# Transposes of the last layer's tokens in four PSUM banks, and the places of some splits and joins in the queues of an attention, experts and MLP kernel

## The chip, the core and the metric

The kernel runs as one program on one core of a Trainium2 chip. The core has a matrix engine (TensorE: PE for matmuls and transposes, PEld for loading the stationary operand), a vector engine (DVE), a scalar engine (ACT), GpSimd (POOL) and SyncE (SP), which here issues nearly all plain DMAs. Each engine works through its own queue in program order; semaphores make one wait for another. A matmul writes to a PSUM bank of 128 x 512 float32. The metric is the time of one execution on the device in microseconds (us), as the median of several.

## The reference: what is computed

Three layers follow one another. Attention over (batch 4, heads 8, 768 positions, 64 wide) with 4 sink keys and a window of 128:

```
keep = is_sink | in_window
a = softmax(where(keep, q @ k.T / 8, -1e9));  x = a @ v     # 3072 tokens x 512
```

Then a mixture of 8 experts, in which each token with `x @ w_skip > 0` goes to the expert with the largest logit, and its result is added to the token:

```
h = relu(x[mask] @ w1[e]);  out[mask] = x[mask] + gate_w * (h @ w2[e])     # 512 -> 1024 -> 512
```

Last an MLP over all 3072 tokens:

```
h = x @ w_in;  r = relu(h);  g = r * r;  return g @ w_out     # 512 -> 2048 -> 512
```

The kernel keeps float32 accuracy by splitting each operand into a high part (rounded by a cast on ACT) and a low part (the difference, by a subtraction on DVE), and by summing three products: high x high, low x high, high x low.

## The kernel before

**Attention (up to about 225 us)** writes its tokens, in blocks of 128, to a buffer in DRAM, `xbuf`. While its last blocks finish, the early expert `e` is worked on in the same queues; the string `Z['chain']` gives the order of all these steps. In it `g0` to `g15` are quarters of the first matmul of `e`, `h0` to `h3` quarters of its second, `m` prepares one part of an expert's weights (`pump(1)`: cast on ACT, subtraction on DVE, then the next weight load on SP), `P` joins the token numbers of the next block on DVE and starts its gather on POOL. The chain ends at a branch on all engines (`tc.If(odd_v > 0)`, line 1102) that is not taken.

**The experts (264 to 424 us)** come in pairs, `units`: a `Pair` has 256 tokens, a `Block` 128. A unit gathers its rows from `xbuf` (`gather`, POOL), transposes them on PE and splits them (`tx`), multiplies with w1 (`g1`), transposes the result where it is a `Block` (`th`, tiles `tph`, `b_hh`, `b_hl`), multiplies with w2 (`g2`), adds the tokens on DVE (L220) and scatters them back to `xbuf` on POOL (L222) in `store`. Between these calls `pump(n)` puts n weight parts into the queues of ACT and DVE. In the last loop `u0` is the pair E-2, `u1` the block E-1, and `u2` one more block of an early expert.

**The MLP.** Its weights come packed as int64 words. `turn(u)` moves a short line of weight tiles on by one step each: `guard` (DVE), `low` (DVE), `begin` (DVE and ACT), `join` (DVE and ACT), `add` (POOL), `high` (ACT). The tail of the experts is ordered by `Z['tail']`: `G`, `a`, `b` are first matmuls of `u2`, `h` and `k` its transposes, `p` and `q` its second matmul, `t` a `turn()` without a new tile, `l` the load of weight tile 3, `u` `turn(wi[3])`, and `0` to `3` `transpose_x(0, t)`.

The MLP takes the tokens in six groups k of 512, the last group of `xbuf` first. `load_x(k, t)` reads 128 tokens from `xbuf`, `transpose_x(k, t)` transposes them by four PE transposes into one PSUM bank (`tpm`) and splits them in two halves of 128 x 256: cast c=0, subtraction c=0, cast c=1, subtraction c=1. The loads of group 1 stand behind the store of `u2`, since they read what it writes. The first steps are the products of weight tile f with group k, in the order (f, 0) for f = 0 to 3, then (0, k), (1, k) for k = 1 to 5; step s is one `gemm1` of 12 matmuls (L1313), a relu on ACT (L1319), a product on DVE (L1321) and a store. The dictionaries `before` and `after` hang loads and transposes on a step. After step 10 no transposes are left; the rest of the 96 steps and the second matmul (L1365) follow.

PSUM has eight banks of which each tile asks for one by a tag: `sc` has four, `tp` two, `xa` and `xb` one each. A tile whose bank is still being read waits for its readers.

Of the kernel before, what the change touches and what calls it, by code (L numbers as in the profile page):

```python
# [20 lines left out]
P = 128  # L21
B, H, S, D = 4, 8, 768, 64
N, DM, E, FF, DFF = 3072, 512, 8, 1024, 2048
# [21 lines left out]
TINY2 = float.fromhex("0x1.2p-15") ** 2  # L45
G = 512

Z = {'la': [0, 0, 2, 2, 7, 10, 12], 'lb': [4, 5, 14, 16, 19, 22, 24], 'ch': 25, 'rk': 35, 'pl': 36, 'ga': [34, 46, 47, 49], 'rw': [28, 29, 46, 54, 62, 70], 'ro': 53, 'rs': 12, 'rg': 4, 'sc0': 50, 'sc1': 0, 'sc2': 57, 'sc3': 12, 'fc': 47, 's2': 51, 'ei': [-5, -3], 'er': [5, 5], 'p': [3, 10], 'qd': [192, 288], 'lv': 31, 'F': [4, 7, 8, 11, 13], 'A': [0, 8, 1, 0, 0, 4], 'T': [1, 2, 6, 2, 1, 2], 'N': [3, 5, 8], 'chain': 't8 la4 lb0 lb2 la5 la6 lb1 lb3 etx r0 lb4 g0 r3 t9 lb5 lb6 r1 c0 c1 c2 c3 ga0 c4 c5 g1 rk ga1 ga2 p0 p2 p3 p4 ga3 r2 p1 p5 o0 s0 s2 s1 g2 o1 t10 s3 o2 s4 g3 rank o3 N0 s5 g4 R0 i0 N2 t11 g5 g6 g7 g8 g9 g10 X N1 i1 g11 g12 send P g13 g14 h0 g15 m m h1 O m m h2 m P m m m u0 m m i2 h3', 'tail': 'Gathbltpku0123q', 'S': [7, 14, 5], 'qd2': [480, 288], 'lv2': 15, 'e0': 3, 'p2': [3, 8], 'eg': 0}
NG = N // G
NF = DFF // P  # L50

# [2 lines left out]
def attn_moe_mlp(ctx: ExitStack, tc: tile.TileContext, kq, v, vs, n_sink, window, wl, w1, w2, w_in, w_out, out):  # L54
# [16 lines left out]
    def bank(tag, name):  # L71
        return ps.tile([P, 512], F32, name=name, tag=tag, bufs={"sc": 4, "tp": 2}.get(tag, 1))
# [8 lines left out]
    def row_tile(name):  # L81
        return wk.tile([P, DM], F32, name=name, tag="row", bufs=5)
# [19 lines left out]
    def join_ids(loaded):  # L102
        ids, n = loaded
        for k in range(1, TABS):
            nc.vector.tensor_tensor(out=ids[:, 0, 0:n], in0=ids[:, 0, 0:n], in1=ids[:, k, 0:n], op=ALU.bitwise_xor)
        return ids[:, 0]

    def split(dst_hi, dst_lo, src):

        nc.scalar.copy(dst_hi, src)  # L110
        nc.vector.tensor_tensor(out=dst_lo, in0=src, in1=dst_hi.bitcast(F32), op=ALU.subtract)  # L111
# [173 lines left out]
    with tc.manual_schedule():  # L285
# [45 lines left out]
        ei = ac.tile([P, 3, E], I32, name="ei")  # L331
# [412 lines left out]
        def at(t, f, p=PTS - 1):  # L744

            plan.setdefault((t + p // PTS, p % PTS), []).append(f)
# [5 lines left out]
        def plan_finish(b, t):  # L752
# [3 lines left out]
            for fs, ps in (  # L756
                (la, Z['la']), (lb, Z['lb']), (choose, range(Z['ch'], Z['ch'] + 6)), ([rank], (Z['rk'],)),
                (place, range(Z['pl'], Z['pl'] + 6)), (gate, Z['ga']),
            ):
                for f, p in zip(fs, ps, strict=True):  # L760
                    at(t, f, p)
            for k, (f, g) in enumerate(rws):
                p = Z['rw'][k] if b == B - 2 else Z['ro'] + Z['rs'] * k
                at(t, f, p)
                at(t, g, p + Z['rg'])
            for k, f in enumerate(scat):
                at(t, f, Z['sc0'] + Z['sc1'] * k if b == B - 2 else Z['sc2'] + Z['sc3'] * k)
# [15 lines left out]
        for n in range(1, B * NP):  # L783
            t, a = n * NQ, (n // NP, n % NP)
# [9 lines left out]
        for t in range(len(units) + 4):  # L794
# [84 lines left out]
        def prep():  # L879

            r = seq[len(units)]
            if r == E:
                units.append(Block(eids[1], 0, etiles, EROWS))
            else:
                ids = ids_of[r] = join_ids(ids_of[r])
                if r in seq[0:3]:

                    own = ids[:, 0:ALLOC[r], 0]
                    nc.vector.tensor_scalar(own, own, nowhere, None, op0=ALU.max)
                units.append(Pair(ids, chunk) if ALLOC[r] == 2 else Block(ids, 0, etiles if len(units) == E - 1 else single_tiles))  # L890
            return units[-1]
# [9 lines left out]
        def send(most=10):  # L901
            while sent[0] < min(len(parts), most - sent[0] % 2):
                r, i = parts[sent[0]]
                if r not in wts_of:
                    if r < E:
                        regs(r)
                    wts_of[r] = Expert(wpa if seq.index(r) % 2 else wpb, e_r[r] if r < E else ew[1], stage)
                wts_of[r].load(i)
                sent[0] += 2

        def pump(n):
            for k in range(n):
# [14 lines left out]
        g1 = [lambda c=c, p=p: e.g1(w_e, c, p, 4) for c in range(4) for p in range(4)]  # L927
        g2 = [lambda p=p: e.g2(w_e, p, 4, False) for p in range(4)]
# [236 lines left out]
        wi = [Unpack(True, f) for f in range(NF)]  # L1165
# [3 lines left out]
        def turn(u=None, between=None):  # L1169

            line.append(u)
            if line[-3]:
                line[-3].guard()
            if line[-4]:
                line[-4].low()
            if u:
                u.begin()
            if between:
                between()
            if u:  # L1180
                u.join()
            if line[-2]:
                line[-2].add()
            if line[-3]:
                line[-3].high()
# [3 lines left out]
        def x_tile(k, a, c):  # L1189
            if k < 2:  # L1190
                return big_tile(4 * k + 3 + 2 * a + c, "xt", F32R)
            return wpb.tile([P, 2, 512], F32R, name=f"w{4 * (k - 2) + 2 * a + c}")

        def load_x(k, t):
            r0 = order[k] * G + t * P
            xgs[k, t] = row_tile("xg") if k == 0 else wpa.tile([P, DM], F32, name="xg", tag=f"w{8 + 4 * (k % 2) + t}")
            nc.sync.dma_start(xgs[k, t], xbuf[r0:r0 + P, :])

        def transpose_x(k, t):
            if t == 0:  # L1200
                xts[k] = [[x_tile(k, a, c) for c in range(2)] for a in range(2)]
            xg = xgs.pop((k, t))
            tp = bank(("sc", "xa", "tp", "tp")[t] if k == 0 else "xa" if t % 2 else "xb", "tpm").rearrange("p (k c) -> p k c", k=4)
            for c in range(4):
                nc.tensor.transpose(tp[:, c, :], xg[:, c * P:(c + 1) * P], ident)  # L1205
            for c in range(2):
                split(xts[k][0][c][:, :, t * P:(t + 1) * P], xts[k][1][c][:, :, t * P:(t + 1) * P], tp[:, 2 * c:2 * c + 2])

        order = [NG - 1] + list(range(NG - 1))
        def wt(n):  # L1210
            return wts_of[seq[n]]

        for n in range(0, E - 2, 2):
            u0, u1 = units[n], units[n + 1]
# [29 lines left out]
        u0, u1, u2 = units[E - 2], units[E - 1], None  # L1244
        for c in range(4):
            u0.g1(wt(E - 2), c)
            pump(4)
            if c == 2:
                u1.tx()
        prep()  # L1250
        for c in range(2):
            u1.g1(wt(E - 1), c)
# [13 lines left out]
        turn(wi[0])  # L1266
        u2.tx()
        u1.g2(wt(E - 1), 1, 2)
        turn(wi[1])
        turn(wi[2])  # L1270
        u1.store()
        for t in range(4):
            load_x(0, t)
        acts = {
            "G": lambda: u2.g1(wt(E), 0), "a": lambda: u2.g1(wt(E), 1, 0, 2), "b": lambda: u2.g1(wt(E), 1, 1, 2),
            "h": lambda: u2.th(0), "k": lambda: u2.th(1), "p": lambda: u2.g2(wt(E), 0, 2, "xb"), "q": lambda: u2.g2(wt(E), 1, 2, "xb"),
# [7 lines left out]
        before, after = {}, {}  # L1284

        def on(when, s, f):
            when.setdefault(s, []).append(f)

        on(before, 0, u2.store)
        for k in range(1, NG):  # L1290
            for t in range(4):
                on(before, 0 if k == 1 else 2 * k - 2, lambda k=k, t=t: load_x(k, t))
                on(after, 2 * k if k > 1 else 2, lambda k=k, t=t: transpose_x(k, t))

        enter = []
        for f in range(4, NF):
# [59 lines left out]
        for s in range(BEHIND, len(steps) + 2 * LOADS):  # L1356
            if s - 2 * LOADS >= 0:
                k, f = steps[s - 2 * LOADS]
# [8 lines left out]
                if f == NF - 1:  # L1367
                    for t in range(4):
# [8 lines left out]
                        r0 = order[k] * G + t * P  # L1377
# [54 lines left out]
```

## Time and profile before

| | us |
|---|---|
| median of 3 runs | 998.36 (996.07 to 1000.64) |
| the profiled execution | 999.1 |
| its span, first to last instruction | 997.4 |
| PE busy | 947.2 (95% of the span) |
| DVE busy | 531.3 (53%) |
| ACT busy | 436.2 (44%) |
| POOL busy | 126.7 (13%) |

The chain of work that ended last is 67% PE; it starts at the branch, at 264.5 us. PE has few gaps left: the profile's 40 slices show it below 90% at three places, the start, the stretch around the branch, and the change from the experts to the MLP at 400 to 490 us. From 491.72 us on PE is busy to the end. In the rows below, a row of the timeline gives start, duration, engine, line, operation, output<-inputs, shapes, count, and in brackets the idle time of the engine before it and who ended it. `SPq` is a DMA being issued, `PEclk` the granted clock of TensorE as a share of full speed.

### The profile page before, as it was taken

What the parts mean: (1) busy time and instruction counts of PE and PEld (TensorE: products, weight loads), DVE (VectorE), ACT (ScalarE), POOL (GpSimd) and SP (SyncE); (2) the same over time, 40 slices, a digit from 0 to 9 for tenths busy, and PEclk for the clock granted to TensorE, in tenths of its full rate; (3) what the DMA queues carried; (4) which work ended last, traced back from release to release, by engine and by line L of the source; (5) the groups of instructions that cost most, each with busy time, mean ns of one, the idle gap of its engine ahead of it and who ended that gap; (6) DMA issues with size and microseconds to landing.
All of it is one profiled execution on the core that took longest, in us unless ns stands there. A gap on an engine that the chain in (4) does not pass through costs nothing.

```text
span 997.4 us, 15187 instructions
## 1 busy us (share of the span) xinstructions
PE 947.2 (95%) x5259; PEld 744.2 (75%) x5259; DVE 531.3 (53%) x1269; ACT 436.2 (44%) x1031; POOL 126.7 (13%) x186
## 2 busy tenths in 40 slices
PE   7999999977799999978799999999999999999998
PEld 4666666657589888756688888888888888888886
DVE  6566677845598798744464555555332232323231
ACT  5766666743276465533443444444232222222221
POOL 3101112122212211200021212112000000000000
PEclk9999999989799999999999999999999999999999
DMA  5433545543698888355354544454353443434231
GB/s 178 146 105 100 145 143 147 177 102 107 221 311 269 287 291 285 133 159 173 110 185 142 176 160 158 154 176 155 116 189 86 149 144 91 144 91 141 85 127 43
DMA packets 90408, 157.17 MB, mean 158 GB/s; under 512 B 14630, under 2 KB 35750, under 8 KB 90322
## 3 DMA queue, kind: packets, MB, share of 16 engines
q1 hardware_dynamic: 87154, 149.11, 46.6%
q0 software_dynamic: 3168, 7.01, 2.1%
q8 instruction: 43, 0.70, 0.3%
q14 instruction: 43, 0.35, 0.1%
HBM read 114.67 MB, written 42.30 MB: 157 GB/s over the span
## 4 chain that ended last, share of the span: by engine, by line
PE 67%; DVE 2%; issue 2%; ACT 1%; DMA 1%; POOL 0%; SPq 0%; POOLq 0%; DVEq 0%; ACTq 0%
PE hpm L1313 27%; PE acc L1365 26%; PE yp L275 4%; PE hp L257 4%; PE hp L197 2%; PE yp L217 2%; PE tpm L1205 1%; DVE w L145 1%; DMA w<-in_w_in_dram 1%; PE tph L206 0%; DVE xt L111 0%; PE tpx L244 0%; ACT xt L110 0%; DVE ua L1140 0%; DVE ua L1146 0%
## 5 line engine op out<-in xcount | busy, mean ns | idle before, releaser
L1365 PE MATMUL acc<-w,gs 128*128 128x512 f32 x1152 | 263.8, 391 | 0.0
L1365 PEld LDWEIGHTS acc<-w,gs 128*128 128x128 f32 x1152 | 216.3, 188 | 47.4
L1313 PE MATMUL hpm<-w,wi 128*128 128x512 f32 x720 | 171.0, 396 | 0.0
L111 DVE TENSOR_TENSOR gs<-g,gs 128x512 fp32r<-128x512 f32 x96 | 66.3, 693 | 177.0 <-ACT gs L110 177.0
L1313 PEld LDWEIGHTS hpm<-w,wi 128*128 128x128 f32 x720 | 135.1, 188 | 32.4
L110 ACT CAST gs<-g 128x512 fp32r<-128x512 f32 x96 | 59.2, 619 | 184.2 <-PE acc L1365 183.7
L1321 DVE SCALAR_TENSOR_TENSOR r<-hpm,r 128x512 f32<-128x512 f32 x96 | 66.3, 691 | 134.1 <-ACT r L1319 134.1
L1319 ACT ACTIVATE r<-hpm 128x512 f32<-128x512 f32 x96 | 57.4, 598 | 165.0 <-PE hpm L1313 165.0
L145 DVE TENSOR_TENSOR w<-wst,w 128x512 fp32r<-128x512 f32 x160 | 103.4, 687 | 16.0 <-ACT w L141 14.9
L468 DVE CUSTOM_DVE_ANT_0 pt<-sc,m 128x272 f32<-128x272 f32 (+2 forms) x192 | 73.4, 409 | 52.5 <-PE sc L457 37.5
L477 ACT ACTIVATE pt<-pt,nm 128x272 f32<-128x272 f32 (+2 forms) x192 | 94.0, 493 | 5.5 <-DVE nm L468 5.5
L141 ACT CAST w<-wst 128x512 fp32r<-128x512 f32 x142 | 81.1, 620 | 25.7 <-DMA wst<-in_w_dram 17.5
L1313 PE MATMUL hpm<-xt,wi 128*128 128x512 f32 x360 | 89.3, 404 | 3.0 <-ACT xt L110 3.0
L1313 PEld LDWEIGHTS hpm<-xt,wi 128*128 128x128 f32 x360 | 69.3, 193 | 20.3 <-ACT xt L110 3.4
L457 PE MATMUL sc<-kq 64*128 64x272 f32 (+2 forms) x384 | 68.1, 433 | 6.0 <-DMA kq<-in_kq_dram 5.9
L1151 POOL TENSOR_TENSOR ua<-ua,ur 128x512 uint32<-128x512 uint32 x32 | 44.6, 1394 | 227.8 <-DVE ua L1146 178.4
L540 PE MATMUL xacc<-pT,vt 128*64 128x128 f32 x704 | 60.4, 289 | 2.6 <-DMA vt<-in_v_dram 1.5
L512 PE MATMUL tp<-ident,pt 128*128 128x128 f32 x352 | 59.1, 287 | 0.0
L512 PEld LDWEIGHTS tp<-ident,pt 128*128 128x128 f32 x352 | 38.2, 142 | 26.2 <-ACT pt L477 12.2
L540 PEld LDWEIGHTS xacc<-pT,vt 128*64 128x64 f32 x704 | 37.1, 137 | 19.3 <-issue 14.3
L257 PE MATMUL hp<-x,w 128*128 128x256 f32 x384 | 47.7, 282 | 0.4 <-DVE x L111 0.4
L257 PEld LDWEIGHTS hp<-x,w 128*128 128x128 f32 x384 | 46.6, 188 | 1.0 <-DVE x L111 0.7
(226 smaller groups left out, 1043.1 us busy)
## 6 DMA issues: line engine op xcount, KB each, us to landing
wst<-in_w_dram SPq DMA_DIRECT2D x80, 512.0 KB, 4.9
gbuf<-r SPq DMA_DIRECT2D x96, 256.0 KB, 2.1
g<-gbuf SPq DMA_DIRECT2D x48, 512.0 KB, 3.7
kq<-in_kq_dram SPq DMA_DIRECT2D x15, 800.0 KB, 4.7
w<-in_w_out_dram SPq DMA_DIRECT2D x16, 512.0 KB, 3.8
wi<-in_w_in_dram SPq DMA_DIRECT2D x15, 512.0 KB, 4.6
vt<-in_v_dram SPq DMA_DIRECT2D x16, 384.0 KB, 5.2
xbuf<-x_sb SPq DMA_DIRECT2D x24, 256.0 KB, 4.4
```

The source lines that it names most:

```text
L111: nc.vector.tensor_tensor(out=dst_lo, in0=src, in1=dst_hi.bitcast(F32), op=ALU.subtract)
L141: copy(self.s[i][:, 0], self.raw[i])
L145: eng.tensor_tensor(out=s[:, 1], in0=self.raw.pop(i), in1=s.bitcast(F32)[:, 0], op=ALU.subtract)
L257: nc.tensor.matmul(self.hp[:, f * 2 * P:(f + 1) * 2 * P], wt.s[c // 2 * 4 + k][:, b, col:col + P], self.x[k // 2][a][:, k % 2 * 2 * P:(k % ...
L457: nc.tensor.matmul(sc[:, 0:wn], kq_sb[own, KW + i * P:KW + (i + 1) * P], kq_sb[own, k0:k0 + wn], start=True, stop=True)
L468: nc.vector.tensor_tensor_reduce(out=pt[:, h, 0:wn], in0=score[u][h][:, 0:wn], in1=(m0, m1, m2)[min(i, 2)], scale=-0.125, scalar=3.0e38, o ...
L477: nc.scalar.activation(out=pt[:, h, 0:wn], in_=pt[:, h, 0:wn], func=AF.Exp, bias=nm[:, h:h + 1], scale=-1.0, accum_out=ssum[:, b, 2 * pr + ...
L512: nc.tensor.transpose(tp[:, h, j, :], pt[:, h, c0:c0 + P], ident)
L540: nc.tensor.matmul(x[h * D:h * D + D, c * P:(c + 1) * P], vv[:, jb, h * D:h * D + D], pT[:, h, j, :], start=j == 0 and (own or first), sto ...
L1313: nc.tensor.matmul(hp, w[:, a, c], x[c // 2][:, c % 2], start=n == 0, stop=n == 11)
L1321: turn(u, lambda: nc.vector.scalar_tensor_tensor(out=r, in0=hp, scalar=0.0, in1=r, op0=ALU.max, op1=ALU.mult))
L1365: nc.tensor.matmul(acc[k][t], g[:, a, t * P:(t + 1) * P], w[:, b], start=f == 0 and n == 0, stop=f == NF - 1 and n == 2)
```

## The change

Six edits, all of order or of place; no arithmetic changes.

```diff
-Z = {... 'chain': '... g12 send P g13 g14 h0 g15 m m h1 O m m h2 ...', 'tail': 'Gathbltpku0123q', ...}
+Z = {... 'chain': '... g12 send g13 g14 g15 h0 m m P h1 O m m h2 ...', 'tail': 'Gathbltpk0123uq', ...}
...
-            tp = bank(("sc", "xa", "tp", "tp")[t] if k == 0 else "xa" if t % 2 else "xb", "tpm").rearrange("p (k c) -> p k c", k=4)
+            tp = bank("sc" if k == 0 and t == 0 else ("xb", "xa", "tp", "tp")[t], "tpm").rearrange("p (k c) -> p k c", k=4)
...
             u0.g1(wt(E - 2), c)
-            pump(4)
             if c == 2:
                 u1.tx()
+            pump(4)
...
             u0.g2(wt(E - 2), p, 4)
-            if p == 1:
+            if p == 0:
                 u1.th(0)
                 u1.th(1)
             pump(6)
...
         u1.g2(wt(E - 1), 1, 2)
-        turn(wi[1])
-        turn(wi[2])
         u1.store()
         for t in range(4):
             load_x(0, t)
+        turn(wi[1])
+        turn(wi[2])
...
-                on(after, 2 * k if k > 1 else 2, lambda k=k, t=t: transpose_x(k, t))
+                on(after, 2 if k == 1 else 2 * k - 1 + t // 2, lambda k=k, t=t: transpose_x(k, t))
```

The transposes of groups 2 to 5 now stand two by two behind two steps in a row, and each of the four tiles of a group has a bank of its own. On PE, before, from the last step of group 0 with three others around it (`x16` are the 16 transposes of one group):

```order
L1313 MATMUL hpm<-xt,wi 128x512 x36
L1205 MATMUL tpm<-ident,xg 128x128 x16
L1313 MATMUL hpm<-xt,w_11977 128x512 x12
L1313 MATMUL hpm<-xt,wi 128x512 x12
L1205 MATMUL tpm<-ident,xg 128x128 x16
L1313 MATMUL hpm<-xt,wi 128x512 x12
```

And in the changed kernel at the same place:

```order
L1313 MATMUL hpm<-xt,wi 128x512 x36
L1205 MATMUL tpm<-ident,xg 128x128 x16
L1313 MATMUL hpm<-xt,w_11977 128x512 x12
L1205 MATMUL tpm<-ident,xg 128x128 x8
L1313 MATMUL hpm<-xt,wi 128x512 x12
L1205 MATMUL tpm<-ident,xg 128x128 x8
L1313 MATMUL hpm<-xt,wi 128x512 x12
L1205 MATMUL tpm<-ident,xg 128x128 x8
```

Group 1 keeps its 16 in one piece; group 2 comes in two pieces of 8, the first of them one step earlier. On DVE, in the tail of the experts, before, from the low part of the tokens of `u2` (`b_xl`) to the low part of its first transposed half (`b_hl`); L1140 and L1146 are `begin` and `join`, L1155 `guard`, L1162 `low`, L220 the add of `u1`'s store:

```order
L111 TENSOR_TENSOR b_xl<-tpx,b_xh 128x512
L1140 TENSOR_SCALAR ua<-wi 128x512
L1146 SCALAR_TENSOR_TENSOR ua<-wi,ua 128x512
L1155 SCALAR_TENSOR_TENSOR ua<-sq,ua 128x512
L1140 TENSOR_SCALAR ua<-wi 128x512
L1146 SCALAR_TENSOR_TENSOR ua<-wi,ua 128x512
L220 SCALAR_TENSOR_TENSOR b_xs<-yp,ids,b_xs 128x512
L1155 SCALAR_TENSOR_TENSOR ua<-sq,ua 128x512
L1162 TENSOR_TENSOR wi<-ua,wi 128x512
L111 TENSOR_TENSOR b_hl<-tph,b_hh 128x512
```

And now:

```order
L111 TENSOR_TENSOR b_xl<-tpx,b_xh 128x512
L220 SCALAR_TENSOR_TENSOR b_xs<-yp,ids,b_xs 128x512
L1140 TENSOR_SCALAR ua<-wi 128x512
L1146 SCALAR_TENSOR_TENSOR ua<-wi,ua 128x512
L1155 SCALAR_TENSOR_TENSOR ua<-sq,ua 128x512
L1140 TENSOR_SCALAR ua<-wi 128x512
L1146 SCALAR_TENSOR_TENSOR ua<-wi,ua 128x512
L1155 SCALAR_TENSOR_TENSOR ua<-sq,ua 128x512
L1162 TENSOR_TENSOR wi<-ua,wi 128x512
L111 TENSOR_TENSOR b_hl<-tph,b_hh 128x512
```

The add of `u1`'s store has moved ahead of five instructions of the weights' line, and with it, on POOL, its scatter ahead of the first two `add`s; the four loads of group 0 on SP stand in the same order as before and wait for that scatter. On ACT, where the second half of the pair's w2 product runs, before (L141 casts weights, L199 is the relu of `u1`, L110 the high part):

```order
L199 ACTIVATE b_hsb<-hp 128x512
L141 CAST w_11606<-wst 128x512
L141 CAST w_11609<-wst 128x512
L141 CAST w_11614<-wst 128x512
L141 CAST w_11639<-wst 128x512
L141 CAST w_11642<-wst 128x512
L141 CAST w_11645<-wst 128x512
L141 CAST w_11648<-wst 128x512
L141 CAST w_11651<-wst 128x512
L141 CAST w_11654<-wst 128x512
L110 CAST b_hh<-tph 128x512 x2
```

And now:

```order
L199 ACTIVATE b_hsb<-hp 128x512
L141 CAST w_11606<-wst 128x512
L141 CAST w_11609<-wst 128x512
L141 CAST w_11614<-wst 128x512
L110 CAST b_hh<-tph 128x512 x2
L141 CAST w_11655<-wst 128x512
L141 CAST w_11658<-wst 128x512
```

The two casts of `u1`'s transposed half have moved ahead of six weight casts, and the two subtractions on DVE ahead of the six that go with them. Of the other moves no row is shown: `u1.tx()` stands ahead of four weight parts (ACT and DVE), `u` behind the splits of group 0 (ACT and DVE), `P` three DVE instructions later, and `g15` ahead of `h0` on PE.

## Rows read from the trace of the kernel before

**Rows 1.** Stretches: us; busy us of PE, PEld, DVE, ACT, POOL; PEclk, DMA, GB/s.

```profile
415.18:434.68 19.50, 14.84 (x73) 11.21 (x72) 11.85 (x20) 8.44 (x18) 4.03 (x3) 0.99 0.26 83
434.68:444.81 10.13, 10.13 (x38) 8.00 (x39) 4.12 (x8) 2.07 (x4) 2.31 (x2) 0.84 0.45 125
444.81:449.27 4.46, 2.11 (x17) 1.69 (x16) 2.60 (x6) 2.54 (x7) 0.00 (x0) 1.00 0.98 327
449.27:491.72 42.45, 32.29 (x162) 25.85 (x161) 19.04 (x42) 16.85 (x43) 1.26 (x1) 0.96 0.43 147
491.72:997.40 505.68, 501.44 (x2173) 407.61 (x2171) 198.74 (x306) 162.43 (x279) 37.86 (x27) 1.00 0.41 135
```

**Rows 2.** Waits of PE, 376 to 492 us: total us, times, longest.

```profile
PE tpm L1205 <- issue: 7.9, 4, 2.6
PE hpm L1313 <- ACT xt L110: 3.0, 1, 3.0
PE tpm L1205 <- DVE xt L111: 1.8, 1, 1.8
PE hp L197 <- DVE b_xl L111: 1.5, 1, 1.5
PE yp L217 <- DVE b_hl L111: 1.2, 2, 1.0
```

**Rows 3.** The chain that ended last, pieces of group 2: start us, us, what.

```profile
449.27 5.55 PE hpm L1313 x24
454.83 0.89 PE tpm L1205 x8
455.72 1.77 issue
```

**Rows 4.** Timeline of ACT and DVE behind the step that ends at 454.83 us.

```profile
454.87 0.60 ACT L1319 ACTIVATE r<-hpm 128x512 f32<-128x512 f32 x1 [2.20 <-PE hpm L1313]
456.11 0.42 DVE L111 TENSOR_TENSOR w<-tpm,w 128x256 fp32r<-128x256 f32 x1
458.15 0.83 DVE L111 TENSOR_TENSOR w<-tpm,w 128x256 fp32r<-128x256 f32 x2 [0.44 <-ACT w L110]
```

**Rows 5.** Timeline of the last experts' loop, 385 to 408 us.

```profile
386.66 0.68 DVE L263 SCALAR_TENSOR_TENSOR h2l<-hp,h2h 128x512 fp32r<-128x512 f32 x1
389.67 0.68 DVE L111 TENSOR_TENSOR b_xl<-tpx,b_xh 128x512 fp32r<-128x512 f32 x1
403.16 4.12 ACT L141 CAST w<-wst 128x512 fp32r<-128x512 f32 x6 [5.02 <-PE yp L275]
407.18 1.06 ACT L110 CAST b_hh<-tph 128x512 fp32r<-128x512 f32 x2
```

**Rows 6.** Timeline from the experts' tail to the MLP, 413 to 440 us.

```profile
413.45 1.34 POOL L1151 TENSOR_TENSOR ua<-ua,ur 128x512 uint32<-128x512 uint32 x1
413.83 1.25 DVE L1140 TENSOR_SCALAR ua<-wi 128x512 uint32<-128x512 uint32 x1
419.51 1.19 POOL L222 DMA_INDIRECT xbuf<-b_xs,ids  x1 [1.95 <-DVE b_xs L220]
422.07 2.08 SPq L1197 DMA_DIRECT2D xg<-xbuf  x4
430.75 0.36 ACT L110 CAST xt<-tpm 128x256 fp32r<-128x256 f32 x1
435.92 0.74 DVE L220 SCALAR_TENSOR_TENSOR b_xs<-yp,ids_e,b_xs 128x512 f32<-128x512 f32 x1
439.71 1.75 SPq L1197 DMA_DIRECT2D xg<-xbuf  x4
```

**Rows 7.** The tile xg over the whole span: its loads, from issue to landing.

```profile
DMA to landing us min/median/max: 2.6/4.0/5.5
```

**Rows 8.** Timeline around the branch, 240 to 265 us.

```profile
249.84 5.78 PE L275 MATMUL yp<-w,w 128*128 128x512 f32 x17 [3.99 <-DVE w L263]
264.62 0.77 PE L197 MATMUL hp<-w,b_xh 128*128 128x512 f32 x1 [5.76 <-DVEq L1102]
```

More of the change, by code (lines that the diff above doesn't have):

```diff
@@ L46 @@
 G = 512
-Z = {'la': [0, 0, 2, 2, 7, 10, 12], 'lb': [4, 5, 14, 16, 19, 22, 24], 'ch': 25, 'rk': 35, 'pl': 36, 'ga': [34, 46, 47, 49], 'rw': [28, 29, 46, 54, 62, 70], 'ro': 53, 'rs': 12, 'rg': 4, 'sc0': 50, 'sc1': 0, 'sc2': 57, 'sc3': 12, 'fc': 47, 's2': 51, 'ei': [-5, -3], 'er': [5, 5], 'p': [3, 10], 'qd': [192, 288], 'lv': 31, 'F': [4, 7, 8, 11, 13], 'A': [0, 8, 1, 0, 0, 4], 'T': [1, 2, 6, 2, 1, 2], 'N': [3, 5, 8], 'chain': 't8 la4 lb0 lb2 la5 la6 lb1 lb3 etx r0 lb4 g0 r3 t9 lb5 lb6 r1 c0 c1 c2 c3 ga0 c4 c5 g1 rk ga1 ga2 p0 p2 p3 p4 ga3 r2 p1 p5 o0 s0 s2 s1 g2 o1 t10 s3 o2 s4 g3 rank o3 N0 s5 g4 R0 i0 N2 t11 g5 g6 g7 g8 g9 g10 X N1 i1 g11 g12 send P g13 g14 h0 g15 m m h1 O m m h2 m P m m m u0 m m i2 h3', 'tail': 'Gathbltpku0123q', 'S': [7, 14, 5], 'qd2': [480, 288], 'lv2': 15, 'e0': 3, 'p2': [3, 8], 'eg': 0}
+Z = {'la': [0, 0, 2, 2, 7, 10, 12], 'lb': [4, 5, 14, 16, 19, 22, 24], 'ch': 25, 'rk': 35, 'pl': 36, 'ga': [34, 46, 47, 49], 'rw': [28, 29, 46, 54, 62, 70], 'ro': 53, 'rs': 12, 'rg': 4, 'sc0': 50, 'sc1': 0, 'sc2': 57, 'sc3': 12, 'fc': 47, 's2': 51, 'ei': [-5, -3], 'er': [5, 5], 'p': [3, 10], 'qd': [192, 288], 'lv': 31, 'F': [4, 7, 8, 11, 13], 'A': [0, 8, 1, 0, 0, 4], 'T': [1, 2, 6, 2, 1, 2], 'N': [3, 5, 8], 'chain': 't8 la4 lb0 lb2 la5 la6 lb1 lb3 etx r0 lb4 g0 r3 t9 lb5 lb6 r1 c0 c1 c2 c3 ga0 c4 c5 g1 rk ga1 ga2 p0 p2 p3 p4 ga3 r2 p1 p5 o0 s0 s2 s1 g2 o1 t10 s3 o2 s4 g3 rank o3 N0 s5 g4 R0 i0 N2 t11 g5 g6 g7 g8 g9 g10 X N1 i1 g11 g12 send g13 g14 g15 h0 m m P h1 O m m h2 m P m m m u0 m m i2 h3', 'tail': 'Gathbltpk0123uq', 'S': [7, 14, 5], 'qd2': [480, 288], 'lv2': 15, 'e0': 3, 'p2': [3, 8], 'eg': 0}
 NG = N // G
```

## Prediction

> **What bounds the kernel now.** I read the busy times of PE by stretch first. From 491.72 us to the end PE is busy for 501.4 of 505.7 us, at the full clock [rows 1]: whatever arrives earlier there arrives earlier at the end, us for us. So the question is how much PE waits in the stretches that the change touches, and what it will wait for instead. Two stretches stand out. In 449.27 to 491.72, groups 2 to 5 of the last layer, PE is busy for 32.3 of 42.5 us; in 415.18 to 434.68, the entry to that layer, for 14.8 of 19.5 [rows 1]. The list of PE's waits names them: 7.9 + 1.8 us ahead of transposes (tpm), 3.0 ahead of the first matmul of the layer, 1.5 for `b_xl`, 1.2 for `b_hl` [rows 2]. The chain of waits shows the pattern of one group: 8 transposes in 0.89 us, then 1.77 us of nothing [rows 3]: the third tile's bank is the first tile's, still being split.
>
> **The change, part by part.** The sum is made against the profiled execution, 999.1 us, with 997.4 of span and 1.7 around it; it stands 0.74 above the median of 998.36.
>
> (1) `u1.tx()` ahead of four weight parts. Now `b_xl` starts on DVE at 389.67, behind four subtractions; moved up it follows `h2l`, which ends at 387.34 [rows 5], and is done at 388.0. PE gets there at 388.4. The 1.5 us [rows 2] go, and about 0.2 for the high part: -1.7. The four weight parts come 0.7 us later; no wait of PE names them.
>
> (2) `u1.th` ahead of six weight casts. These casts wait for PE to free the weights' places (5.02 us) and run until 407.28; only then come the casts of `b_hh` [rows 5]. Moved, they run right behind their transposes, beside the 36 matmuls of the pair that PE still has. The longest of the 1.2 us, and 0.2 for the high part, go: -1.2. The six casts are themselves held by PE, not by the queue, so nothing is late behind them.
>
> (3) The entry, counted from the end of `u1`'s last matmul, now 415.18. Before, the first matmul of the layer comes 19.5 us later [rows 1]. After: add of the store 0.74, issue of the scatter 1.19, and now only the first `add` on POOL, 1.34 [rows 6]: 3.35. `guard` takes 0.7, and on ACT a `begin`, a square, a `high` and the relu of `u2` follow at 0.6 each, the `begin` having waited for that `add`: 5.85. PE has done its 18 matmuls (0.231 each, 24 in 5.55 [rows 3]) by 4.15: a new wait of 1.7. Transposes and 6 matmuls take it to 7.75; the low part of its next operand comes at 8.3, behind a `begin` that takes 1.25 beside POOL's `add` [rows 6]: another 0.35. Then 12 matmuls and 4 transposes: 11.3. The tokens' loads are issued 2.56 after the scatter starts [rows 6], at 3.4, and the fourth has landed by 10.3 even at the longest 5.5 [rows 7]: no wait where 1.5 us were. The splits begin at 11.9 instead of waiting behind weight tile 3, and the layer's first matmul starts 3.93 after the first cast (430.75 to 434.68 [rows 1, 6]) plus 0.3 for a subtraction in front: 16.1. So -3.4. By PE's own busy 14.84 plus the new 2.3 it would be 17.1, -2.4; with the new waits half as long -4.5.
>
> (4) The 36 matmuls after this take 10.13 us at a granted 0.84, behind a wait of 3.0 [rows 1, 2]; at full rate 8.32. The wait in front shrinks to about 0.2, as those of 0.35 and less elsewhere at 1.00: -1.8 (none if the clock falls all the same).
>
> (5) Group 1. Before, its transposes take 4.46 us [rows 1], against 1.78 at 0.89 per 8. The bank wait, 2.7, goes. But what is late next? Its loads follow the scatter of `u2`. Counted from the layer's first matmul, the last split ends at 1.24 (435.92 - 434.68); then `low`, `begin` and `join` of weight tile 3, put there by the change, 1.8; the add 0.74; to the first load 3.05 (436.66 to 439.71 [rows 6]): 6.85. The fourth load is issued 1.3 later and lands 2.6, 4.0 or 5.5 after that [rows 7]: 10.8, 12.2 or 13.7. Its transposes end 0.45 later; without waits they would have at 10.1. A wait of 1.1, 2.5 or 4.0 takes the place of 2.7: I take the middle, -0.2, between -1.6 and +1.3. The Trainium skill, page "DMA: Bandwidth & Descriptors", section "Anatomy of one DMA", gives 2.0 us plus the bytes at 436 GB/s for one transfer: an estimate of 2.6 us for 256 KB, as the shortest landing here; by it the wait would be 1.1 and the time 976.
>
> (6) Groups 2 to 5: 42.45 us. PE's work is 8 steps of 2.78 and 8 times 0.89: 29.3. Do the splits keep up with one step and two tiles every 3.67 us? Behind the step that ends at 454.83 the relu starts at once, the first subtraction at 456.11, and the fourth, the last of two tiles, ends at 458.57, 3.7 us after the step [rows 4]; the next product needs DVE only 0.6 into the next step. So they just fit. A group's last tiles are ready 3.7 after their step and wanted 0.89 + 2.78 + 0.89 = 4.56 after it. Loads of group k are issued some 1.7 us after step 2k-3 and wanted 7.3 after it; at the longest 5.5 [rows 7] they are there. 0.4 for one step with a weight tile in between: -12.7 (bounds -9 and -13.1).
>
> (7) `P` behind two weight parts, `g15` ahead of `h0`. PE loses a wait of 3.99 us, but then all engines meet at the branch, where PE already idles 5.76 [rows 8]; the branch is left when the last table loads on SP land, and DVE's work in front of those is not moved. I take 0; the gain would be 4.0 at most, a loss 1.
>
> Sum: 1.7 + 1.2 + 3.4 + 1.8 + 0.2 + 12.7 = 21.0. 999.1 - 21.0 = 978.1, and 977.4 beside the median; I forecast 977.5.
>
> **The rivals.**
> - Entry lost: POOL's three scatters each wait for the one before, and the `add`s now stand behind the third; if that third is issued 5 us later than I count, (3) and (4) go to zero. For it: POOL's place in the chain above. Against it: the one in the rows let the loads behind it go 2.56 us after its start [rows 6]. 977.5 + 5.2 = 982.7.
> - Clock. The stretch 449.27 to 491.72 was granted 0.96 and the one before it 1.00 [rows 1], so the clock fell somewhere among transposes and waits, and group 1 keeps such a place: 4 us of transposes and waits in front of a step. If it falls there, some 3.5 us of matmuls take twice as long: +1.7, 979.2; with a second fall 981. The Trainium skill, page "TensorE: Matmul & The Clock Gate", section "Part 4: PE-mode transpose", says that transposes don't count as activity for the clock; that speaks for this rival, and the 1.00 of 444.81 to 449.27 with 2.1 us of transposes in it neither confirms nor refutes it.
> - The wait isn't the bank. If the pair of ACT and DVE is the limit in (6), two tiles at a time move the wait from the transposes to the next step. For it: they just fit. Then about half of (6) stays: 984.
> - The branch gives: (7) passes it, 973.5.
> - Slower: the loads of groups 2 to 5 have one step less between issue and use. From a landing of about 5.6 us on each further us is paid four times; 26 us of loss over my forecast take a landing of 12 us, over twice the longest [rows 7]. For it: stores of 256 KB share the queues. Above 1003.
>
> **How the numbers follow.** Forecast 0.62, entry lost 0.10, clock 0.13, ACT and DVE 0.06, branch 0.06, slower 0.02; 0.01 that nothing changes. The forecast's own range is 974.5 to 980.5, from the bounds of (3), (5) and (6). For 8 in 10 I take 973 to 985, the branch and the rivals up to ACT and DVE within it. 0.5% is 5 us, about what a measurement of this kernel tells: below 993.4 is faster, 0.96; the same 0.02; slower 0.02.
>
> **What would show it.** In the new profile: no wait of PE for `b_xl` before `u1`'s first matmul; none for `b_hl` before its w2; a wait of about 1.7 us ahead of `tph` of `u2`; the layer's first 36 matmuls in some 8.3 us; group 1's transposes waiting for xg instead of a bank; then 8 steps and 64 transposes in about 30 us with no gap above 0.5. Wrong: a new gap of several us ahead of the first matmul of a group, PE below 90% there, or a DMA named by the waits of groups 2 to 5.

## The result, and the profile after

The changed kernel takes 980.5 us (978.37 to 982.51, 4 runs) against 997.22 (993.37 to 1000.64, 4 runs) of the kernel before beside it: ratio 0.9835, 95% interval 0.9807 to 0.9862. A second comparison gave 980.91 us and 0.9815 (0.9785 to 0.9845). The forecast was 977.5 with a range of 973 to 985: faster, as predicted, and 3 us less of it than predicted, at the upper end of the forecast's own 974.5 to 980.5. The gain between medians measured side by side is 16.7 and 17.6 us (998.51 to 980.91), where 20.9 were predicted.

The profiled execution took 979.77 us, 19.3 less than that of before. This table splits the difference. Each stretch runs from the start of one PE instruction in the timeline to the start of another; only the first two rows meet at a scatter on POOL. The names A to E are used below.

| stretch | before | after | difference | predicted |
|---|---|---|---|---|
| start to the first scatter of the early expert's table (`tab`) | 232.29 | 230.59 | -1.70 | 0 |
| from there, past the branch, to the first transposes after it (`tpx`) | 57.39 | 55.54 | -1.85 | 0 (7) |
| the experts, to A, the end of `u1`'s last matmul | 125.50 | 122.04 | -3.46 | -2.9 (1, 2) |
| A to B, the layer's first matmul: the entry | 19.50 | 19.86 | +0.36 | -3.4 (3) |
| B to C, the transposes of group 1: 36 matmuls | 9.96 | 9.60 | -0.36 | -1.8 (4) |
| C to D, group 1 | 4.39 | 4.42 | +0.03 | -0.2 (5) |
| D to E, groups 2 to 5 | 42.45 | 29.97 | -12.48 | -12.7 (6) |
| E to the end | 505.92 | 505.98 | +0.06 | 0 |

The busy times by stretch, from A, of the changed kernel (columns as in [rows 1], whose stretches of before have the same names and ends up to 0.24 us later than the table's):

```profile
408.17:428.03 19.86, 15.58 (x74) 12.37 (x72) 11.48 (x18) 7.45 (x16) 4.99 (x4) 0.91 0.28 86
428.03:437.63 9.60, 8.93 (x37) 6.70 (x37) 5.85 (x11) 3.91 (x7) 2.30 (x2) 1.00 0.28 83
437.63:442.05 4.42, 2.84 (x16) 2.43 (x17) 2.35 (x6) 1.76 (x5) 0.00 (x0) 0.77 1.02 318
442.05:472.02 29.97, 29.97 (x162) 25.16 (x161) 17.29 (x40) 14.77 (x40) 0.00 (x0) 0.98 0.65 217
472.02:978.00 505.98, 501.77 (x2175) 407.83 (x2173) 200.34 (x309) 164.21 (x283) 39.05 (x28) 1.00 0.41 135
```

Groups 2 to 5 have no idle PE left, where they had 10 us; the entry still idles 4.3 us. The list of PE's waits from 376 to 475 us is down from [rows 2] to two entries:

```profile
PE tph L206 <- ACT b_hsb L199: 4.2, 1, 4.2
PE tpm L1205 <- DMA xg<-xbuf: 2.2, 3, 1.3
```

The waits for `b_xl`, `b_hl` and the banks are gone. The casts of `b_hh`, at 407.18 behind six others in [rows 5], now stand in their place on ACT, and the two subtractions soon behind them:

```profile
393.97 1.07 ACT L110 CAST b_hh<-tph 128x512 fp32r<-128x512 f32 x2
395.77 1.28 DVE L111 TENSOR_TENSOR b_hl<-tph,b_hh 128x512 fp32r<-128x512 f32 x2
```

The chain of waits shows groups 2 to 5, beside [rows 3]: where 8 transposes were followed by 1.77 us of nothing, the next step follows at once, eight times over.

```profile
440.46 1.94 PE tpm L1205 x8
442.40 3.30 PE hpm L1313 x12
445.70 0.87 PE tpm L1205 x8
446.57 2.80 PE hpm L1313 x12
...
471.39 0.87 PE tpm L1205 x8
472.27 237.84 PE hpm L1313 x1020
```

Group 1 now waits for its loads, 2.2 us in all, and its step runs 3.30 instead of 2.80: the granted clock stood at 0.77 in the stretch ahead of it. The loads land in this time (that of [rows 7] was 2.6/4.0/5.5):

```profile
DMA to landing us min/median/max: 3.0/3.7/4.4
```

The entry is where a wait of 4.2 us has come in. Its timeline, as in [rows 6]:

```profile
407.03 0.98 POOL L222 DMA_INDIRECT xbuf<-b_xs,ids  x1 [2.50 <-DVE b_xl L111]
...
408.37 0.75 DVE L220 SCALAR_TENSOR_TENSOR b_xs<-yp,ids,b_xs 128x512 f32<-128x512 f32 x1 [1.34 <-PE yp L217]
...
411.35 0.97 POOL L222 DMA_INDIRECT xbuf<-b_xs,ids  x1 [3.34 <-DMA xbuf<-b_xs,ids]
...
412.34 2.51 POOL L1151 TENSOR_TENSOR ua<-ua,ur 128x512 uint32<-128x512 uint32 x2
413.65 0.66 ACT L1141 ACTIVATE ur<-wi 128x512 uint32<-128x512 uint32 x1 [6.34 <-POOL ua L1151]
...
413.68 2.07 SPq L1197 DMA_DIRECT2D xg<-xbuf  x4
...
416.02 0.59 ACT L199 ACTIVATE b_hsb<-hp 128x512 f32<-128x512 f32 x1
...
416.66 1.12 PE L206 MATMUL tph<-ident,b_hsb 128*128 128x128 f32 x4 [4.19 <-ACT b_hsb L199]
```

The add of `u1`'s store runs right at A, as the change wants it. But its scatter is not issued at 409.1: POOL waits 3.34 us until the scatter before it, issued at 407.03, has landed. The weights' first `add` stands behind it and starts at 412.34, where POOL was free for it from 408.01 (407.03 + 0.98). ACT's next `begin` waits for that `add`, 6.34 us, and the relu of `u2` (L199) stands behind it on ACT; PE waits for the relu. [Rows 6] of before has the opposite order on POOL: `add` at 413.45, scatter at 419.51. Note that the scatter's own record is short, 0.98 us, and its landing 3.34 us later shows only as another's wait. That is what the Trainium skill, page "Perfetto Trace Analysis", section "DMA Instruction — SWDGE (GPSIMD)", says of such a DMA: its end in the profile is that of writing the descriptors, not of moving the data. The trace agrees.

At the branch the wait of 3.99 us in [rows 8] is gone from the matmuls, and one of 4.86 us for a gather stands a little later:

```profile
252.96 1.09 PE L183 MATMUL tpx<-ident,s_xs 128*128 128x128 f32 x4 [4.86 <-DMA s_xs<-xbuf,ids]
261.94 0.47 PE L197 MATMUL hp<-w,b_xh 128*128 128x512 f32 x1 [4.31 <-DVEq L1102]
```

### The profile page after: what moved, and what is told of

It is laid out like the page before. It is cut to its first block, busy times and chain, and to the rows that moved or that the text cites. A ratio compares the mean times of both kernels' runs of the same rounds, so it can differ in the third digit from the quotient of the medians.

```text
span 978.0 us, 15186 instructions
## 1 busy us (share of the span) xinstructions
PE 942.7 (96%) x5259; PEld 743.2 (76%) x5259; DVE 531.3 (54%) x1269; ACT 436.2 (45%) x1031; POOL 125.8 (13%) x186
## 4 chain that ended last, share of the span: by engine, by line
PE 55%; issue 2%; DMA 0%; POOL 0%; DVE 0%; ACT 0%; POOLq 0%; ACTq 0%
PE acc L1365 27%; PE hpm L1313 27%; PE tpm L1205 1%; DMA xg<-xbuf 0%; POOL ua L1151 0%; POOL xbuf L222 0%; DVE ua L1155 0%; ACT w L1159 0%; DVE ob L1372 0%; ACT ob L1371 0%; POOLq L1151 0%; POOLq L222 0%; ACTq L1159 0%
## 5 line engine op out<-in xcount | busy, mean ns | idle before, releaser
L110 ACT CAST gs<-g 128x512 fp32r<-128x512 f32 x96 | 59.4, 621 | 184.0 <-PE acc L1365 183.6
L141 ACT CAST w<-wst 128x512 fp32r<-128x512 f32 x142 | 81.5, 621 | 28.4 <-DMA wst<-in_w_dram 24.9
L1313 PE MATMUL hpm<-xt,wi 128*128 128x512 f32 x360 | 87.1, 396 | 0.0
```

What stands on the lines that cost most here:

```text
L141: copy(self.s[i][:, 0], self.raw[i])
L1313: nc.tensor.matmul(hp, w[:, a, c], x[c // 2][:, c % 2], start=n == 0, stop=n == 11)
```

## The experiments

Eleven runs were made, each with a profile and against the kernel before. The stretches of all of them, in us from the profiles, cut as in the table above:

| kernel | experts | A-B | B-C | C-D | D-E | A-E |
|---|---|---|---|---|---|---|
| before | 125.50 | 19.50 | 9.96 | 4.39 | 42.45 | 76.30 |
| changed | 122.04 | 19.86 | 9.60 | 4.42 | 29.97 | 63.85 |
| changed, second profile | 122.04 | 21.08 | 9.42 | 4.20 | 30.88 | 65.58 |
| banks and two by two alone | 127.28 | 19.38 | 9.87 | 1.66 | 30.05 | 60.96 |
| banks alone | 127.22 | 19.09 | 10.03 | 1.76 | 32.53 | 63.41 |
| two by two alone | 125.62 | 19.47 | 8.79 | 4.39 | 29.35 | 62.00 |
| store undone | 122.04 | 19.13 | 8.40 | 2.30 | 29.35 | 59.18 |
| `u` undone | 122.04 | 22.74 | 10.33 | 1.67 | 29.35 | 64.09 |
| both undone | 122.03 | 21.05 | 10.34 | 1.67 | 29.33 | 62.39 |
| first turn ahead, `u` late | 122.04 | 17.27 | 8.78 | 3.24 | 29.36 | 58.65 |
| store taken apart | 122.04 | 15.26 | 9.48 | 4.10 | 29.36 | 58.20 |
| store taken apart, `u` late | 122.04 | 15.24 | 8.78 | 3.40 | 29.35 | 56.77 |
| old chain | 122.04 | 19.47 | 9.36 | 4.86 | 29.89 | 63.58 |

### The transposes: which edit did it

On top of the kernel before, the last edit alone, and its two halves:

```diff
+# banks alone, and in banks and two by two
+            tp = bank("sc" if k == 0 and t == 0 else ("xb", "xa", "tp", "tp")[t], "tpm")...
+# two by two alone, and in banks and two by two
+                on(after, 2 if k == 1 else 2 * k - 1 + t // 2, lambda k=k, t=t: transpose_x(k, t))
```

Banks and two by two. Expected:

> The kernel before with the last edit alone: four banks for the transposes of groups 1 to 5, and groups 2 to 5 two by two. Theory (terms 5 and 6 stand by themselves): groups 2 to 5 go from 42.45 us to some 30, as they did in the changed kernel (30.2), group 1 loses its bank wait and gains a wait for its loads of 1 to 4 us, between 0 and -2.6; in all -12 to -15, 982 to 985 us, ratio 0.985 to 0.988. Rival (the pace of the pair ACT and DVE was eased by the other edits): half of it stays, a gap in front of every second step, 990 us.

Measured 984.26 us, ratio 0.985 (0.9814 to 0.9886), and 30.05 us for groups 2 to 5; group 1 in 1.66. As the theory had it, but group 1 waits for no load: PE comes to it 7.6 us behind the issue of `u2`'s scatter (437.06, 444.67), in the changed kernel 5.7 (431.95, 437.63).

Two by two alone. Expected:

> The kernel before with the transposes of groups 2 to 5 two by two, but in the two old banks. Theory (the placement alone would do): a pair uses each of the two banks once and comes back to them 3.67 us later, when the second tile's splits have just ended (3.7 us): waits of at most 0.3 us a pair, groups 2 to 5 at 30 to 33 us; group 1 keeps its bank wait of 2.7; 985 to 988 us. Rival (four banks are needed): each pair waits 1 us or more for its second bank, groups 2 to 5 at 37 us or more, 991 us or more.

Measured 987.45 us, 0.9882 (0.985 to 0.9915). PE from group 1 on:

```profile
445.07 0.63 PE L1205 MATMUL tpm<-ident,xg 128*128 128x128 f32 x4 [1.78 <-DVE xt L111]
446.26 0.63 PE L1205 MATMUL tpm<-ident,xg 128*128 128x128 f32 x4 [0.56 <-PE tpm L1205]
446.65 3.00 PE L1313 MATMUL hpm<-xt,w 128*128 128x512 f32 x12
449.49 1.03 PE L1205 MATMUL tpm<-ident,xg 128*128 128x128 f32 x8
450.28 3.04 PE L1313 MATMUL hpm<-xt,wi 128*128 128x512 f32 x12
```

Groups 2 to 5 run at 29.35 without one wait: in the two old banks. The four banks are not needed there. They are worth the 1.78 and 0.56 us inside group 1, whose 16 transposes stand in one piece.

Banks alone. Expected:

> The kernel before with the four banks, but the 16 transposes of a group still in one piece behind one step. Theory (the banks and the two by two are both needed): the 1.77 us of bank wait inside each of the groups 2 to 5 go, but a group's last tiles are wanted one step after their transposes, 1.78 + 2.78 = 4.56 us, and the splits of four tiles take some 5 us and the relu and its product stand between: a new wait of 1 to 2 us ahead of the first product of each group. Groups 2 to 5 at 34 to 38 us, the kernel at 988 to 993 us. Rival (the banks are the whole cause): groups 2 to 5 at 30 to 31 us, 983 to 985 us.

Measured 988.21 us, 0.9891 (0.9859 to 0.9924), 32.53 us for groups 2 to 5, and 507.58 instead of 505.92 from E to the end. No wait inside a group is left, and one ahead of a step has taken its place:

```profile
451.08 1.91 PE L1205 MATMUL tpm<-ident,xg 128*128 128x128 f32 x16
452.74 3.03 PE L1313 MATMUL hpm<-xt,wi 128*128 128x512 f32 x12
456.05 3.35 PE L1313 MATMUL hpm<-w,wi 128*128 128x512 f32 x12 [0.28 <-ACT w L110]
...
481.33 6.14 PE L1313 MATMUL hpm<-w,wi 128*128 128x512 f32 x24 [1.07 <-ACT w L110]
```

The wait is there as expected, but 0.2 to 0.3 us a group and once 1.07, not 1 to 2. A step starts on the first cast of the last tile (ACT is what the wait names); I had priced it as if it needed all the splits. The step behind the wait takes 3.2 us instead of 2.8, and the longest wait lies behind E: of the 9.9 us that groups 2 to 5 gain, 1.7 are lost again there, and 8.3 are kept. Two by two alone takes 13.1 us off, the banks alone 8.3, both together 12.4: the halves do not add.

The changed kernel beside them. Expected:

> The changed kernel itself, beside the three others on the same chip: 978 to 983 us. Its trace is a second one of the new chain: if the 3.55 us that it was early at the first transposes behind the branch (303.3 us, before 306.9) come from P and g15, these transposes start at 303 to 304 us here too, and at 306 to 307 in the three kernels with the old chain; if they are the spread of the attention from run to run, the four times mix.

Measured 980.91 us. Its `tpx` came at 287.32, those of the three others at 288.14, 286.59 and 288.38 (the transposes that the expectation counts come 17.20 us later in each): the four mix, and the times of arrival are no evidence for the chain (it has a run of its own below).

### The entry: what the scatter holds

The changed kernel with the store edit undone:

```diff
         u1.g2(wt(E - 1), 1, 2)
+        turn(wi[1])
+        turn(wi[2])
         u1.store()
         for t in range(4):
             load_x(0, t)
-        turn(wi[1])
-        turn(wi[2])
```

> The changed kernel with the store edit undone: the two steps of the weights' line stand ahead of u1's add, scatter and loads again; u stays behind the splits. Counted from the end of u1's last matmul to the layer's first matmul, the changed kernel took 19.86 and 21.08 us in two traces, the kernel before 19.50. Theory (the third scatter waits 3.34 us for the second one's landing, and the adds behind it hold ACT and by that PE): no wait ahead of u2's tph, 16 to 17 us for the entry, since the splits no longer wait behind weight tile 3; group 1 still waits about 2 us for its loads; 977 to 979 us, 3 below the changed kernel. Rival (the store edit gives the 2 to 3 us that I had put on it, and something else ate them): the entry at 21 us or more, 982 to 984 us.

Measured 975.63 us, 0.9772 (0.9751 to 0.9794); A to E 59.18 instead of 63.85 and 65.58. The `add`s run at A, ACT has its relu done at 411.49, PE starts `tph` at 411.54, and the list of waits has no entry there:

```profile
407.15 2.57 POOL L1151 TENSOR_TENSOR ua<-ua,ur 128x512 uint32<-128x512 uint32 x2
...
408.51 0.67 ACT L1141 ACTIVATE ur<-wi 128x512 uint32<-128x512 uint32 x1 [2.25 <-POOL ua L1151]
...
410.90 0.59 ACT L199 ACTIVATE b_hsb<-hp 128x512 f32<-128x512 f32 x1
...
411.26 0.75 DVE L220 SCALAR_TENSOR_TENSOR b_xs<-yp,ids,b_xs 128x512 f32<-128x512 f32 x1
411.54 0.66 PE L206 MATMUL tph<-ident,b_hsb 128*128 128x128 f32 x4
...
420.31 0.63 PE L1205 MATMUL tpm<-ident,xg 128*128 128x128 f32 x4 [1.36 <-DMA xg<-xbuf]
...
435.84 1.33 PE L1205 MATMUL tpm<-ident,xg 128*128 128x128 f32 x8 [0.17 <-DMA xg<-xbuf]
```

The theory stands in that the wait of 4.2 us is gone, with two misses: the entry is 19.13, not 16 to 17, and the time lies below its 977 to 979. The add now comes at 411.26, behind a guard on DVE that waits for POOL, so the scatter and the loads are later, the third tile's transposes wait 1.36 us for them, and the twelve matmuls behind take 4.4 us (421.80 to 426.23) instead of 3.0 in the changed kernel (425.04 to 428.03). So of the 4.7 us only 0.7 come in the entry; 1.2 come from B to C, 2.1 in group 1 and 0.6 behind it. The splits of group 0 are done before B here, and `u2`'s scatter is issued 1.23 us behind B (427.46) instead of 3.92 (431.95), so that PE waits 0.17 us for group 1's loads instead of 2.2.

`u` undone, and both undone. The first is the string `Gathbltpku0123q` in the changed kernel, the second adds the edit just shown. Expected:

> The changed kernel with weight tile 3 (u) ahead of the splits of group 0 again; the store edit stays. Theory (the wait at the scatter ate the gain of both edits): the 4.2 us wait ahead of u2's tph stays, the splits wait for weight tile 3 besides if its load lands late; the entry at 20 to 22 us; but u2's add and scatter stand 1.6 us nearer to the last split, so group 1 waits 0.5 to 1 us instead of 2.2; within 1 us of the changed kernel, 979 to 982 us. Rival (moving u is what costs): the entry at 19 us or less and group 1 without a wait, 977 us.

> The changed kernel with the store edit and u undone: what is left are the four banks, the two by two, tx and th, and the chain. From the end of u1's last matmul to the last transposes' end the changed kernel took 63.85 and 65.58 us, the kernel before with banks and two by two alone 60.96. Theory (store and u together cost 3 us): 61 us here too, all else as in the changed kernel, so 977 to 978 us, ratio about 0.979. Rival (the two edits are worth nothing either way, and the difference is where the clock fell): 980 to 982 us.

Measured 980.88 us, 0.9809 (0.9786 to 0.9832), and 978.64 us, 0.978 (0.9753 to 0.9807). The first is as expected in the time: with the store edit in place `u` changes nothing (64.09 from A to E). The entry, 22.74, is above the expected 20 to 22, and group 1 loses its wait entirely (1.67). The second fell outside its theory: 62.39 us from A to E, not 61. With the store undone, `u` behind the splits is worth 62.39 - 59.18 = 3.2 us; against the kernel with banks and two by two alone, which has the same order there, 60.96 - 59.18 = 1.8. So the store edit costs, and `u` gains where the scatter does not eat it. For `u` this is likely and not shown: the two medians differ by less than their intervals tell, and the stretches are of one profile each, with 1.4 us between the two of the same order and 2.0 among the changed kernel's two and the old chain's below.

The order `add`, scatter, `add`, and `u` late:

```diff
+        turn(wi[1])
         u1.store()
         for t in range(4):
             load_x(0, t)
-        turn(wi[1])
         turn(wi[2])
...
         on(before, 0, u2.store)
+        on(before, 0, lambda: turn(wi[3]))
```

> The changed kernel with the order on POOL add, scatter, add (turn of weight tile 1 ahead of u1's store, that of tile 2 behind), and u behind u2's store instead of ahead of it. Theory (the first add must stand ahead of the scatter that waits): the first add runs while the scatter waits anyway, ACT gets to u2's relu in time, the 4.2 us wait ahead of tph shrinks to under 1; the entry 16 to 17 us; u2's scatter goes 1.6 us earlier, so group 1 waits 0.5 to 1; 58 to 60 us from u1's last matmul to the last transposes, 974 to 976 us. Rival (the loads of group 0 behind the scatter become the next wait, or the second add does): the entry stays at 19 us or more, 978 us or more.

Measured 978.09 us, 0.978 (0.9757 to 0.9803). The entry is 17.27, near the theory, and 58.65 us from A to E are within it; the time lies above its 974 to 976, and the rival's second `add` is there too. The scatter is issued at 415.47, the second `add` behind it, then guard and `high`, and `b_hh` of `u2` stands behind that `high` on ACT:

```profile
416.48 2.52 POOL L1151 TENSOR_TENSOR ua<-ua,ur 128x512 uint32<-128x512 uint32 x2
...
419.59 0.62 ACT L1159 CAST wi<-ua 128x512 fp32r<-128x512 f32 x1 [3.65 <-DVE ua L1155]
...
420.75 0.50 PE L217 MATMUL yp<-w,b_hh 128*128 128x512 f32 x1 [2.38 <-ACT b_hh L110]
```

Its profile reached the first scatter of `tab` at 234.82, the latest of all, so the profile's total says less than the stretch; that does not explain the median.

The store taken apart, its add on DVE early and its scatter on POOL behind both `add`s; then the same with `u` late:

```diff
     def store(self):
+        self.join()
+        self.scatter()
+    def join(self):
         nc.vector.scalar_tensor_tensor(...)
+    def scatter(self):
         nc.gpsimd.indirect_dma_start(...)
...
-        u1.store()
+        turn(wi[1])
+        u1.join()
+        turn(wi[2])
+        u1.scatter()
         for t in range(4):
             load_x(0, t)
-        turn(wi[1])
-        turn(wi[2])
```

> The changed kernel, but u1's store is taken apart: its add on DVE stands between the two steps of the weights' line, its scatter on POOL behind both adds. In the kernel with the store edit undone the scatter was issued 5.2 us after the end of u1's last matmul, since DVE's add stood behind a guard that waits for POOL, and group 0's last two loads were 1.8 us late; there the entry took 19.1 us and the twelve matmuls behind the wait ran partly at half rate. Theory (the scatter can go as soon as the one before it has landed, some 3.2 us after that end): loads 2 us earlier, no wait for them, the entry at 16 to 17.5 us, 57 to 58 us from u1's last matmul to the last transposes, 973 to 975 us. Rival (landing of loads and splits, not the scatter, sets the first matmul): the entry at 18.5 or more, 975 to 977 us.

> The same, and u moved behind u2's store. Theory (where the entry is shorter, u's low, begin and join, 1.8 us of DVE, stand ahead of u2's add): group 1 waits 1 to 2 us less for its loads than in the kernel with the store taken apart and u ahead; 972 to 974 us. Rival (weight tile 3 is then late for its step, the fourth of the layer): a new wait ahead of the matmuls behind group 1, 975 us or more.

Measured 975.12 us, 0.9752 (0.9729 to 0.9775), and 974.54 us, 0.9753 (0.9729 to 0.9778). The entry of the first:

```profile
409.63 2.58 POOL L1157 TENSOR_TENSOR ua<-ua,ur 128x512 uint32<-128x512 uint32 x2
409.78 0.75 DVE L224 SCALAR_TENSOR_TENSOR b_xs<-yp,ids,b_xs 128x512 f32<-128x512 f32 x1 [0.28 <-PE yp L217]
...
412.65 0.99 POOL L228 DMA_INDIRECT xbuf<-b_xs,ids  x1 [0.44 <-issue]
...
415.00 2.07 SPq L1203 DMA_DIRECT2D xg<-xbuf  x4
...
419.88 2.22 PE L1211 MATMUL tpm<-ident,xg 128*128 128x128 f32 x16
```

The scatter is issued 3.1 us behind A (409.58), the entry has no wait for a load and takes 15.26 us, below the forecast's 16.1. PE waits 2.4 us for the loads of group 1, and 1.3 with `u` late: 1.1 less, at the low end of 1 to 2. Both times lie just above what their theories said (973 to 975, 972 to 974). Both lie clearly below the changed kernel in A to E, by 5.7 and 7.1 us. In the medians the gap is 5.4 and 6.0 us against 980.5, with intervals of the ratio that do not meet; against the store undone (975.63) they are not told apart.

### The branch

The changed kernel with the old chain string, `P` ahead of `g13` and `g15` behind `h0`. Expected:

> The changed kernel with the old chain: P ahead of g13, g15 behind h0. Measured from the first of the six scatters of the early expert's tokens (some 232 us) to the first transposes behind the branch (some 287 us), four traces of the old chain took 57.4, 55.4, 56.2 and 57.6 us, six of the new one 54.4 to 55.6. Theory (my 0 was wrong; the chain gives some 1.5 us, in part by PE's clock behind the branch): 56 to 57.6 here, 981 to 983 us. Rival (the four were high by chance): 54.4 to 55.6, 980 us. Either way the yp wait of 4 us ahead of the branch is back.

Measured 982.83 us, 0.9833 (0.9811 to 0.9854), and 57.44 us; the wait for `w` ahead of the branch is back, 4.7 us. From the `tab` scatter to `tpx`, the five traces of the old chain have 55.40, 56.19, 57.39, 57.44 and 57.59, the eight of the new one 54.42, 54.87, 55.04, 55.37, 55.54, 55.56, 56.86 and 56.94. The means differ by 1.2 us, and the two sets overlap: the two last runs, made after this expectation, have the new chain and lie high. That the chain gives about 1 us is likely and not shown.

## Why the prediction was right, and where it was not

The sum was 978.1, the profile has 979.77. That the two are so near is in part luck, as the end of this list shows. The steps:

- (1) and (2), `tx` and `th`: right. All nine profiles with them take 122.03 or 122.04 us through the experts, the four without 125.50 to 127.28. The terms were 2.9; the two profiles without them in which the clock stayed up give 3.5. No run separates the two terms. In the two others the clock fell behind the wait for `b_xl`, for 1.7 us more.
- (3), the entry: wrong, 0.36 us lost where 3.4 were to be gained, and it is the step that failed. I had the scatter issued as soon as the add in front of it was done, and took the wait for the scatter before it to be over by then. It was issued 3.2 us behind A (411.35 - 408.17), 2.2 us after its data was ready, and "a new wait of 1.7" measured 4.2. The rival called entry lost names this mechanism, three scatters each waiting for the one before and the `add`s behind the third; I gave it 0.10 and asked 5 us of delay for it, but 2.2 sufficed, since two `add`s, ACT's `begin` and the relu queue up behind. Its price, 5.2 us on (3) and (4), is what the two lost (3.8 and 1.4), though by chance in the second part: (4) lost it in other ways, as the next point says. Against it I had set a scatter whose loads follow 2.56 us after its start; that row is of the last scatter, 7.05 us behind the one before it. The rows that would have told, two scatters in close order earlier in the trace of before, 4.66 us apart, I had not read:

```profile
375.78 1.00 POOL L222 DMA_INDIRECT xbuf<-b_xs,ids  x1 [4.68 <-DMA xbuf<-s_xs,ids]
380.44 0.97 POOL L222 DMA_INDIRECT xbuf<-b_xs,ids  x1 [3.66 <-DMA xbuf<-b_xs,ids]
```

- (4), the clock of the first 36 matmuls: 0.36 gained in the stretch, of 1.8. They take 8.93 us at 1.00, so 1.2 came; the rest of the stretch is the first wait for group 1's loads, 0.67. With the store undone, where the last splits are done before B, they take 8.40, near the 8.32 of the sum; in the changed kernel the last splits end at 429.34, 1.3 us behind B. That the shorter wait in front is the reason is not shown: in the kernel with two by two alone these matmuls took 8.95 us behind a wait of 3.3.
- (5), group 1: right. 2.2 us of waits for loads, predicted 2.5, in place of the bank's. The figure that (5) takes from the Trainium skill, page "DMA: Bandwidth & Descriptors", section "Anatomy of one DMA", is given there for a DMA that GpSimd issues; these loads are issued by SP, and the shortest landed after 3.0 us.
- (6), groups 2 to 5: 12.48 of 12.7, right in size. In its reason it was too broad: I took four banks and two by two for one thing. The two by two alone gives all of it; the banks alone 8.3, two thirds.
- (7), the branch: 0 predicted, 1.85 in this pair of profiles, some 1.2 in the means. That PE's wait only moves is what the rows show. The 1.70 us ahead of it, before anything that the change touches, is spread: the `tab` scatter lies between 230.19 and 234.82 over thirteen profiles, with either chain.

What (3) and (4) lost, 5.2 us, was in this profile largely made good by (7) and the early start, 3.55, and by 0.6 in (1) and (2). Of the 3.55, 1.70 arose ahead of anything that the change touches: that is luck. The median is 3 us above the forecast, and that of before, 997.22, is 1.1 below the one that the forecast was made on; side by side 3.3 to 4.2 us of the 20.9 are missing, which is nearer to what (3) and (4) lost.

On the clock, the rival of 0.13: it fell in group 1, as that rival has it. In the first profile only 0.5 to 0.6 us of matmuls were lost to it (3.30 against 2.80, 29.97 against 29.35). In the second, group 1's transposes were granted 0.99 and the step behind them 0.62 (444.06 to 448.50 us), and 1.5 us were lost (30.88 against 29.35), near the rival's 1.7:

```profile
444.06 4.54 PE L1313 MATMUL hpm<-xt,w 128*128 128x512 f32 x12
```

What decides it, no run here settles. In the kernels with banks and two by two, and with two by two alone, PE waits 1.7 us for `b_xl` behind the same work. The 6 us from the end of that wait, first of the one, then of the other:

```profile
389.07:395.07 6.00, 6.00 (x19) 4.78 (x20) 3.85 (x7) 2.23 (x5) 0.00 (x0) 0.72 0.95 311
```

```profile
389.30:395.30 6.00, 6.00 (x26) 4.99 (x27) 5.41 (x10) 3.12 (x6) 0.00 (x0) 1.00 0.87 301
```

A granted clock of 0.72, part of the time at the lower of its two levels, and 1.00: PE gets through 19 matmuls and through 26. The same holds of group 1: 4.42 us of transposes and waits in the changed kernel gave 0.77, 4.39 us with two by two alone 1.00.

## What to carry to other kernels

Before moving an instruction ahead of others in a queue, look for what it waits for at its new place, and price everything that then stands behind it: an indirect scatter that has to wait for the landing of the one before holds its whole queue. If such an operation has two halves on two engines, move the half that is ready and leave the one that waits behind the work that does not. Where transposes feed their own splits, spread them over the steps first; more banks help only where they stand in one piece.

## What the runs showed of the hardware

A scatter to `xbuf` that the profile shows waiting for the one before it was issued 4.32 us after it in the changed kernel (407.03, 411.35) and 4.66 in the kernel before (375.78, 380.44): for 3.34 and 3.66 us of that POOL stood still, whatever was behind. This is not so for every scatter in close order. The scatters to `tab` go to three tables in turn: in the changed kernel the first three were issued at 230.59, 231.92 and 233.28 without such a wait, and the fourth, to the first table again, waited 1.54 us for a landing. So look at whether two scatters write the same tensor. A kernel's arrival at one POOL instruction, 230 us in, spread over 4.6 us between profiles, and from the row of the last table loads (`ids<-tab`, on SP) ahead of the branch to PE's first matmul behind it 1.9 to 3.8 us passed. So a difference of 1 to 2 us is read from a stretch that starts behind such places: the experts' 122.04 us came out within 0.01 in nine profiles.
